# Respacing the filter units of an FFT filter that runs between the matmuls of a GELU MLP

## The chip, the cores and the metric

The kernel runs on one core of a Trainium2 chip. The metric is the time of one execution on the device in microseconds (us), as the median of several runs. A profile is one execution, recorded by the hardware profiler.

## The reference

Eight sequences of 3008 rows and 256 columns are filtered along the rows with a real FFT, a product with a complex filter and the inverse FFT. Each filtered row then goes through an MLP with exact GELU.

```python
X = np.fft.rfft(x, axis=1)                    # x: (8, 3008, 256)
F = (filt_r + 1j * filt_i)[None, :, :]        # (1505, 256)
y = np.fft.irfft(X * F, n=3008, axis=1)
h = y.reshape(24064, 256) @ w_in              # w_in: (256, 2048)
g = 0.5 * h * (1.0 + erf(h / sqrt(2)))
out = g @ w_out                               # w_out: (2048, 256)
```

## The kernel before

**The MLP** is cut into 47 tiles of 512 rows. For each of the 16 blocks of the hidden width, `mm1` (L637) makes two 512-column matmuls into a PSUM bank "h" (three of them), and ScalarE writes the GELU to `g_sb` (L640). The second matmul of a tile, `mm2_seven`, replaces eight block products by seven with sums of its operands: 7 groups m = 0 to 6 of 16 matmuls each (L709), 112 in all. The sums of `g_sb` are made by VectorE in `sums_1` (L678, four a tile), `sums_2` (L684, two) and `sums_3` (L691, two). The results of L709 go into two PSUM banks "o" that alternate: group 0 into one, groups 1 and 2 into the other, 3 and 4 into the first, 5 and 6 into the other. VectorE empties them: L724 after group 0, L726 and L729 after group 2, L731, L732 and L735 after group 4, L738 (two instructions) after group 6. Group 1 of the next tile needs the bank that L738 empties, group 3 the one of L724, group 5 the one of L729.

**The order is a list of slots written out by hand.** Slot s = 16 t + j. In each slot the program first issues what was put there, then 7 matmuls of `mm2_seven` for tile t - 1, then the two matmuls of `mm1` for block j of tile t. So the place of a slot in its tile, j (called phase here), tells which group of L709 runs: group m starts in slot 16 m / 7. Every engine runs its own instructions in this order of issue. Slots 16 to 31 hold a first, plain form of the second matmul (L650, emptied by L654).

**The filter** of batch 0 runs ahead of the slots. Batches 1 to 7 are filtered inside them, each in time for its rows, in steps:

- `fold` (L107, L108): VectorE sums and differences of the loaded rows; four a batch.
- `s1` (L430): 8 matmuls, four a batch; the result goes through `a_sb` to DRAM (`R1`, L439). `r1` (L445) loads it back as `b_sb`, in three loads of 512 KB on the DMA queue of SP.
- `s2` (L457): 32 small matmuls into one bank "h" and three banks "f", for each of three units u. Then `s2_out` (L468), four times a unit: VectorE multiplies a bank with the filter, 128 x 1024 elements, into a tile p. The products are called P1 to P4 here. After P2 and after P4, the same function makes the complex sum of its tile: a subtraction (L471) and an addition (L472).
- `s3` (L485): 24 matmuls of the unit's two tiles p, the first step of the inverse ("inverse burst"), into one bank "h" and the three banks "f". ScalarE empties them (`s3_out`, L326) and SP writes them to DRAM (`R2`, L495). `r2` (L503) loads the result as `d_sb`, four pieces a batch.
- `s4` (L512): 4 matmuls, 16 times a batch, into a bank "f"; ScalarE or VectorE (L326 or L330) writes them to `ring`, where `mm1` reads its rows.
- `load_next`: eight times a batch, the loads of the next batch's rows on the DMA queue of POOL, behind a small copy (`gate`, L146) that waits for one product.

Finished rows leave by `put_rows` (L756) on POOL's queue; of tile 1 three of four pieces go by SP's queue.

**The planner** (the loops over `b` in the kernel's main function) sets the slot of each step from `hi`, the first slot of the first tile that holds rows of batch b: 176, 272, 368, 464, 560 and 656 for b = 2 to 7. In it, `s2` is the triple of slots of the three units, and `s3 = s2[u] + 10` (9 for two units of batch 1). The products stand in slots s2, s2 + 2, s2 + 4 and s2 + 6 (s2, + 2, + 5, + 6 in the second unit of batch 1, one slot later in the first unit of batch 2). `s4` is placed backwards from its due time into slots that are not marked busy, so it moves when `s2` and `s3` move. After the last `s3` of batch b, `after[b]` is the first slot for loads `r2`.

Of the kernel before, what the change touches and what calls it, by code (L numbers as in the profile page):

```python
# [10 lines left out]
ALU = mybir.AluOpType  # L11
# [20 lines left out]
class _Mix:  # L32
# [428 lines left out]
    def s2_out(self, b, u, m, d):  # L461

        if d == 0:
            self.st[b, "p", 2 * u + m] = self.pp.tile([128, 2, 2, 2, 256], BF16, tag="p12", name="p12")
        w, a, v = self.st[b, "p", 2 * u + m], m ^ d, self.nc.vector.tensor_tensor
        ps = self.st[b, "ps2"][m][d].rearrange("p (r c) -> p r c", r=2)
        f = self.Fu[:, :, a, 2 * u + m, :]
        v(out=w[:, a], in0=ps.unsqueeze(2).to_broadcast([128, 2, 2, 256]),  # L468
          in1=f.unsqueeze(1).to_broadcast([128, 2, 2, 256]), op=ALU.mult)
        if d:  # L470
            v(out=w[:, :, 0, 0], in0=w[:, :, 0, 0], in1=w[:, :, 1, 1], op=ALU.subtract)  # L471
            v(out=w[:, :, 0, 1], in0=w[:, :, 0, 1], in1=w[:, :, 1, 0], op=ALU.add)  # L472

    def s3(self, b, u):

# [217 lines left out]
    def mm2_seven(self, t, lo, hi):  # L693

        nc, v = self.nc, self.nc.vector.tensor_tensor
        a11, a12, s2, a22 = self.quarters(t)
        w = self.w_out_sb.rearrange("p (i k) (n o) -> p k n i o", k=2, n=2)
        q = self.w_sums
        s31, s4 = self.st["s", t], self.st.get(("s4", t))
        ops = ((a11, w[:, 0, 0]), (a12, w[:, 1, 0]), (s2, q[:, 1]), (s31[:, :, 0], q[:, 2]),  # L700
               (s31[:, :, 1], q[:, 0]), (a22, q[:, 3]), (s4, w[:, 1, 1]))
        last = t == self.B * self.S // TCH - 1
        for n in range(lo, hi):
            m, sub, i = n // 16, n // 8 % 2, n % 8
            if n % 16 == 0 and (m == 0 or m % 2 == 1) or last and m > 4 and i == 0:
                self.st["o"] = self.bank("ps_o", "h" if n > 80 else "o").rearrange("p (m s o) -> p m s o", m=2, s=2)
            ps = self.st["o"]
            a, b = ops[m]
            nc.tensor.matmul(ps[:, (m + 1) % 2, sub, :], lhsT=a[:, i, 128 * sub:128 * sub + 128], rhs=b[:, i],  # L709
                             start=i == 0, stop=i == 7)  # L710
            if last and m > 4 and i == 7:
                self.finish(t, m, sub, ps)
            if n % 16 != 15 or m % 2 or last and m > 4:
                continue
            p0, p1 = ps[:, 0], ps[:, 1]
            if m == 0:
                self.st["t"] = self.po.tile([128, 2, 2, 128], FP32, tag="ost", name="t_sb")
                self.st["c"] = [None, None]
            if m in (2, 4):
                self.st["c"][m // 4] = self.po.tile([128, 2, 256], FP32, tag="ost", name="ost")  # L720
            t1, t3 = self.st["t"][:, 0], self.st["t"][:, 1]
            c = lambda h, k: self.st["c"][h][:, :, 128 * k:128 * k + 128]
            if m == 0:
                nc.vector.tensor_copy(out=t1, in_=p1)  # L724
            elif m == 2:
                v(out=c(0, 0), in0=t1, in1=p0, op=ALU.add)  # L726
                if last:
                    self.store(t, 0, 0, nc.sync)
                v(out=t1, in0=t1, in1=p1, op=ALU.add)  # L729
            elif m == 4:  # L730
                v(out=t3, in0=t1, in1=p0, op=ALU.subtract)  # L731
                v(out=c(1, 1), in0=t3, in1=p1, op=ALU.add)  # L732
                if last:
                    self.store(t, 1, 1, nc.scalar)
                v(out=t1, in0=t1, in1=p1, op=ALU.add)  # L735
            else:
                for h, tt, p in ((1, t3, p0), (0, t1, p1)):
                    v(out=c(h, 1 - h), in0=tt, in1=p, op=ALU.add)  # L738
                    for sub in range(2):
                        self.put_rows(t * TCH + 256 * h + 128 * sub, self.st["c"][h][:, sub],  # L740
                                      nc.gpsimd if t > 1 or h > sub else nc.sync)

    def put_rows(self, r0, tile_, eng):

# [33 lines left out]
def kernel(  # L778
# [9 lines left out]
    m = _Mix(ctx, tc, x, filt_r, filt_i, moe_w_in, moe_w_out, out)  # L788
    nc, B, S = tc.nc, m.B, m.S
# [116 lines left out]
    def put(slot, f, *a):  # L906
        at.setdefault(slot, []).append((f, a))

    def first(b):
        return (b * S // TCH) * 16  # L910

    busy, crowd, after = set(), set(), {}
    for b in range(1, B):
        hi = first(b)
        e = 4 * (b == B - 1)
        s1, n1, r1 = (4, 2.75, 16) if b == 1 else (hi - 87, 3.7, hi - 73) if b == 2 else (hi - 94 - e, 3.7, hi - 80 - e)
        s2 = (33, 45, 57) if b == 1 else (hi - 64 - 2 * e + (b == 2), hi - 48 - 3 * e + e // 4, hi - 32 - 3 * e)
        busy.update(range(s1 - 1, s1 + int(3 * n1) + 2))
        for c in range(4):
            slot = s1 + int(c * n1 + (b == 1 and c in (1, 2)))  # L920
            put((0, 1, 5, 8)[c] if b == 1 else (67, 69, 86, 94)[c] if b == 2 else s1 - 28 + e + 6 * c, m.fold, b, c)
            put(slot, m.s1, b, c)
        for u in range(3):
            put(r1 if u < 2 else s2[0] + 1, m.r1, b, u)
            put(s2[u], m.s2, b, u)
            for i in range(4):
                put(s2[u] + ((0, 2, 5, 6)[i] if b == u == 1 else 2 * i + (b == 2 and u == 0)), m.s2_out, b, u, i // 2, i % 2)
            s3 = s2[u] + (9 if b == 1 and u != 1 else 10)
            put(s3, m.s3, b, u)
            put(s3 + 1, m.s3_out, b, u, 1)  # L930
            busy.update(range(s2[u] - 1, s2[u] + 5), range(s3 - 1, s3 + 2))
        after[b] = s3 + (5 if b > 1 else 4)
        crowd.update(range(s2[0], after[b]), range(s1 + 66, s1 + 94))
        if b + 1 < B:
            for i, (u, o, p) in enumerate(((0, 5, 1), (0, 7, 1), (1, 1, 2), (1, 5, 3), (1, 7, 3), (2, 1, 4), (2, 5, 5), (2, 7, 5))):
                put(s2[u] + o, m.load_next, b, p, i // 2, i % 2)
# [46 lines left out]
    for s in range((NT + 1) * 16):  # L983
        t, jc = s // 16, s % 16
# [42 lines left out]
```

## Time and profile before

| | us |
|---|---|
| median of 3 runs (750.72 to 751.89) | 751.08 |
| the profiled execution | 750.39 |
| its span, first to last instruction | 748.6 |
| PE busy | 730.8 (98%) |
| DVE (VectorE) busy | 616.9 (82%) |
| ACT (ScalarE) busy | 575.1 (77%) |
| POOL busy | 288.2 (39%) |

In the profile PE is TensorE, PEld its weight loads. A line of the timeline gives start, duration, engine, line of the kernel, operation and operands of an instruction or of equal ones in a row. Instructions of one engine overlap by a little, so a queue without gaps is read by the distance from start to start.

### The profile page before, as it was taken

The page shows a single profiled execution, that of the slowest core. Times are in us where ns is not written, and L with a number is a line of the kernel's source. Part 1 is how long each engine was busy: PE and PEld are TensorE (multiplying, and loading weights), DVE is VectorE, ACT ScalarE, POOL GpSimd, SP SyncE. Part 2 cuts the span into 40 slices and gives each one's busy share as a digit, 9 for nine tenths or more (in the row PEclk, how much of TensorE's full clock was granted, in tenths as well). Part 3 has the DMA queues.
Part 4 walks back from the last instruction along what each step waited for, and adds up shares of the span by engine and source line. Part 5 has one row for each costly group of instructions (what it writes and reads, how often), then busy time and mean ns, then how long its engine had stood idle before and what let it go on. Part 6 is the DMA issues. An engine that isn't in the chain of part 4 may idle for free.

```text
span 748.6 us, 22400 instructions
## 1 busy us (share of the span) xinstructions
PE 730.8 (98%) x9261; PEld 508.9 (68%) x9261; DVE 616.9 (82%) x1120; ACT 575.1 (77%) x1048; POOL 288.2 (39%) x544
## 2 busy tenths in 40 slices
PE   8999999999999999999999999999999999999997
PEld 4856666666777667666677666666767766777776
DVE  8977998899887998789977989769997898676566
ACT  6987777677887788878887777877878787777773
POOL 7893446666122552234431355114631122112121
PEclk9999999999999999999999999999999999999999
DMA  9996542745345552546535455355444433301011
GB/s 154 213 193 185 125 109 86 212 90 123 86 121 177 117 119 82 142 148 134 112 103 162 111 126 131 90 158 129 117 108 118 153 91 99 117 31 58 29 57 58
DMA packets 81353, 89.31 MB, mean 119 GB/s; under 512 B 13171, under 2 KB 60659, under 8 KB 81251
## 3 DMA queue, kind: packets, MB, share of 16 engines
q0 software_dynamic: 22352, 39.76, 23.1%
q1 hardware_dynamic: 58483, 47.93, 22.8%
q8 instruction: 72, 1.18, 0.7%
q14 instruction: 30, 0.25, 0.1%
q10 hardware_dynamic: 416, 0.20, 0.1%
HBM read 55.57 MB, written 48.23 MB: 139 GB/s over the span
## 4 chain that ended last, share of the span: by engine, by line
PE 77%; DVE 15%; DMA 3%; POOL 2%; issue 2%; ACT 0%; DVEq 0%; POOLq 0%; SPq 0%
PE ps_h L637 35%; PE ps_o L709 33%; DVE p L468 5%; DMA x_sb<-in_x_dram 3%; PE ps_s L512 2%; PE ps_s L430 2%; DVE s_sb L678 2%; POOL out_dram L756 1%; PE ps_s L485 1%; DVE p L472 1%; PE ps_s L457 1%; DVE g_sb L684 1%; PE ps_o L650 1%; DVE s_sb L691 1%; DVE x_sb L108 1%
## 5 line engine op out<-in xcount | busy, mean ns | idle before, releaser
L640 ACT ACTIVATE g_sb<-ps_h 128x512 f16<-128x512 f32 x752 | 447.9, 603 | 146.1 <-PE ps_h L637 142.5
L637 PE MATMUL ps_h<-y_sb,w_in_sb 128*128 128x512 bf16 (+3 forms) x1600 | 445.3, 366 | 0.2 <-DVE a_sb L328 0.2
L756 POOL DMA_DIRECT2D out_dram<-ost x228 | 129.4, 574 | 389.3 <-DVE ost L738 359.4
L709 PEld LDWEIGHTS <-g_sb 128*128 128x128 f16 x2944 | 193.9, 98 | 90.1 <-issue 13.5
L709 PEld LDWEIGHTS <-s_sb 128*128 128x128 f16 x2208 | 147.8, 98 | 56.7 <-issue 3.7
L709 PE MATMUL ps_o<-w_sums,g_sb 128*128 128x128 f16 x1472 | 127.5, 219 | 4.7 <-DVE t_sb L729 3.5
L637 PEld LDWEIGHTS <-w_in_sb 128*128 128x128 bf16 x1600 | 125.0, 98 | 8.5 <-issue 1.1
L709 PE MATMUL ps_o<-w_sums,s_sb 128*128 128x128 f16 x1472 | 126.2, 219 | 0.1
L709 PE MATMUL ps_o<-w_out_sb,g_sb 128*128 128x128 f16 x1472 | 119.4, 219 | 2.1 <-DVE ost L738 2.1
L678 DVE TENSOR_TENSOR s_sb<-g_sb 128x1024 f16<-128x1024 f16 x184 | 120.3, 687 | 0.8 <-ACT g_sb L640 0.8
L468 DVE TENSOR_TENSOR p<-ps_s,F 128x1024 bf16<-128x1024 f32 x84 | 102.1, 1217 | 3.5 <-PE ps_s L457 1.8
L99 POOL DMA_DIRECT2D x_sb<-in_x_dram x156 | 79.0, 513 | 2.4 <-DMA x_sb<-in_x_dram 0.8
L684 DVE TENSOR_TENSOR g_sb<-s_sb,g_sb 128x1024 f16<-128x1024 f16 x92 | 65.0, 707 | 1.6
L709 PE MATMUL ps_o<-w_out_sb,s_sb 128*128 128x128 f16 x736 | 63.9, 219 | 0.0
L691 DVE TENSOR_TENSOR s_sb<-g_sb 128x1024 f16<-128x1024 f16 x92 | 63.8, 693 | 0.0
L731 DVE TENSOR_TENSOR t_sb<-t_sb,ps_o 128x256 f32<-128x256 f32 x46 | 19.3, 419 | 40.9 <-PE ps_o L709 39.7
L326 ACT ACTIVATE v_sb<-ps_s 128x512 bf16<-128x512 f32 x83 | 45.5, 608 | 6.3 <-PE ps_s L485 5.7
L326 ACT ACTIVATE y_sb<-ps_s 128x376 bf16<-128x376 f32 x94 | 46.6, 496 | 4.6 <-PE ps_s L512 4.6
L512 PEld LDWEIGHTS <-d_sb 96*128 96x128 bf16 x448 | 31.2, 97 | 27.2 <-issue 2.2
L738 DVE TENSOR_TENSOR ost<-t_sb,ps_o 128x256 f32<-128x256 f32 x90 | 33.7, 415 | 18.1 <-PE ps_o L709 18.1
L328 DVE CAST a_sb<-ps_s 128x512 bf16<-128x512 f32 x54 | 34.7, 684 | 12.7 <-PE ps_s L430 12.4
L726 DVE TENSOR_TENSOR ost<-t_sb,ps_o 128x256 f32<-128x256 f32 x46 | 19.1, 416 | 24.7 <-PE ps_o L709 24.1
(156 smaller groups left out, 556.7 us busy)
## 6 DMA issues: line engine op xcount, KB each, us to landing
out_dram<-ost POOLq DMA_DIRECT2D x126, 128.0 KB, 2.7
b_sb<-R SPq DMA_DIRECT2D x21, 512.0 KB, 5.2
R<-v_sb SPq DMA_DIRECT2D x84, 128.0 KB, 2.6
d_sb<-R SPq DMA_DIRECT2D x56, 192.0 KB, 3.3
R<-a_sb SPq DMA_DIRECT2D x108, 96.0 KB, 2.2
x_sb<-in_x_dram POOLq DMA_DIRECT2D x48, 94.0 KB, 2.7
x_sb<-in_x_dram POOLq DMA_DIRECT2D x48, 48.0 KB, 2.7
x_sb<-in_x_dram POOLq DMA_DIRECT2D x12, 188.0 KB, 5.1
```

The source lines that it names most:

```text
L99: self.nc.gpsimd.dma_start(out=xt[64 * v + to:64 * v + to + m, h, 4 * c:4 * c + 4 * n, :], in_=xv[h][at:at + m, w:w + 4 * n, :])
L326: self.nc.scalar.activation(out=out, in_=in_, func=AF.Copy, scale=1.0 if scale is None else scale)
L328: self.nc.vector.tensor_copy(out=out, in_=in_)
L468: v(out=w[:, a], in0=ps.unsqueeze(2).to_broadcast([128, 2, 2, 256]), in1=f.unsqueeze(1).to_broadcast([128, 2, 2, 256]), op=ALU.mult)
L512: nc.tensor.matmul(ps[:, 94 * i:94 * i + 94], lhsT=d[:, (grp % 2) * 4 + i, 128 * half:128 * half + 128], rhs=self.T4a[:, 4 * grp + i, 0:2 ...
L637: nc.tensor.matmul(ps[:, o:o + n], lhsT=w[:, dc], rhs=self.ring[:, dc, off:off + n], start=(dc == 0), stop=(dc == 1))
L640: nc.scalar.activation(out=self.st["g", t][:, jc, :], in_=ps, func=AF.Gelu)
L678: self.nc.vector.tensor_tensor(out=self.st["s", t][:, i:i + 2], in0=a, in1=b, op=ALU.subtract)
L684: self.nc.vector.tensor_tensor(out=a21[:, k], in0=self.st["s", t][:, k, 0], in1=a22[:, k], op=ALU.add)
L691: self.nc.vector.tensor_tensor(out=self.st["s4", t][:, k], in0=a12[:, k], in1=s2[:, k], op=ALU.subtract)
L709: nc.tensor.matmul(ps[:, (m + 1) % 2, sub, :], lhsT=a[:, i, 128 * sub:128 * sub + 128], rhs=b[:, i], start=i == 0, stop=i == 7)
L756: eng.dma_start(out=out, in_=tile_[lo - r0:lo - r0 + n])
```

## The change

The complex sums leave `s2_out` and become a step of their own, `s2_sum`, one slot behind P2 and one behind P4. The inverse burst stands 13 slots behind its unit (12 in batch 1). The units stand further apart:

| batch | units before | units after | bursts before | bursts after |
|---|---|---|---|---|
| 1 | 33, 45, 57 | 28, 43, 58 | 42, 55, 66 | 40, 55, 70 |
| 2 | 113, 128, 144 | 113, 129, 145 | 123, 138, 154 | 126, 142, 158 |
| 3 to 6 | hi - 64, - 48, - 32 | hi - 72, - 53, - 34 | hi - 54, - 38, - 22 | hi - 59, - 40, - 21 |
| 7 | 584, 597, 612 | 580, 596, 612 | 594, 607, 622 | 593, 609, 625 |

For batches 3 to 6 the phases of the units were 0, 0 and 0; they become 8, 11 and 14. Of batch 1 they were 1, 13 and 9; they become 12, 11 and 10. `r1(b, 2)`, `load_next`, `s4` and `r2` move along, and of the four pieces of tile 1's output one goes by SP's queue instead of three.

```diff
         v(out=w[:, a], in0=ps.unsqueeze(2).to_broadcast([128, 2, 2, 256]),
           in1=f.unsqueeze(1).to_broadcast([128, 2, 2, 256]), op=ALU.mult)
-        if d:
-            v(out=w[:, :, 0, 0], in0=w[:, :, 0, 0], in1=w[:, :, 1, 1], op=ALU.subtract)
-            v(out=w[:, :, 0, 1], in0=w[:, :, 0, 1], in1=w[:, :, 1, 0], op=ALU.add)
+
+    def s2_sum(self, b, p):
+
+        w, v = self.st[b, "p", p], self.nc.vector.tensor_tensor
+        v(out=w[:, :, 0, 0], in0=w[:, :, 0, 0], in1=w[:, :, 1, 1], op=ALU.subtract)
+        v(out=w[:, :, 0, 1], in0=w[:, :, 0, 1], in1=w[:, :, 1, 0], op=ALU.add)
...
-                                      nc.gpsimd if t > 1 or h > sub else nc.sync)
+                                      nc.gpsimd if t > 1 or h * sub == 0 else nc.sync)
...
-        s2 = (33, 45, 57) if b == 1 else (hi - 64 - 2 * e + (b == 2), hi - 48 - 3 * e + e // 4, hi - 32 - 3 * e)
+        s2 = (28, 43, 58) if b == 1 else (hi - 63, hi - 47, hi - 31) if b == 2 else (hi - 72 - e, hi - 53 - 7 * e // 4, hi - 34 - 5 * e // 2)
...
             for i in range(4):
-                put(s2[u] + ((0, 2, 5, 6)[i] if b == u == 1 else 2 * i + (b == 2 and u == 0)), m.s2_out, b, u, i // 2, i % 2)
-            s3 = s2[u] + (9 if b == 1 and u != 1 else 10)
+                put(s2[u] + 2 * i + (b == 2 and u == 0), m.s2_out, b, u, i // 2, i % 2)
+            for i in range(2):
+                put(s2[u] + 3 + 4 * i + (b == 2 and u == 0), m.s2_sum, b, 2 * u + i)
+            s3 = s2[u] + (12 if b == 1 else 13)
...
-        after[b] = s3 + (5 if b > 1 else 4)
+        after[b] = s3 + (5 if 1 < b < B - 1 else 4)
```

Here `e` is 4 for batch 7 and 0 otherwise.

## The prediction

> **What bounds the kernel now.** I read the page's busy times first, then the chain that ended last, then the waits of PE, then the timeline of single units.
>
> ```profile
> PE 730.8 (98%) x9261; PEld 508.9 (68%) x9261; DVE 616.9 (82%) x1120; ACT 575.1 (77%) x1048; POOL 288.2 (39%) x544
> ...
> PE 77%; DVE 15%; DMA 3%; POOL 2%; issue 2%; ACT 0%; DVEq 0%; POOLq 0%; SPq 0%
> ```
>
> PE is the bound, but 15% of the chain is VectorE: in places PE waits for it. How much is read from the slots. Where there is no filter work (660 to 740 us) the `mm1` pairs of neighbouring slots start 0.82 us apart (660.42, 661.24, 662.07), 0.8225 us on average. In the timeline a slot with `s4` is longer by 0.17 us, with `s1` by 0.66, with `s2` by 0.67, with an undisturbed `s3` by 0.68. What a slot takes beyond that is PE's wait. Added up over slots 32 to 640, outside `s1` and tile 5's own slots, the waits are:
>
> | batch | 1 | 2 | 3 | 4 | 5 | 6 | 7 | sum |
> |---|---|---|---|---|---|---|---|---|
> | us | 4.68 | 4.03 | 1.89 | 1.89 | 1.91 | 1.90 | 1.06 | 17.36 |
>
> So 17.4 us is the most that better spacing can bring. In batch 4 the first unit shows where its part comes from. VectorE:
>
> ```profile
> 326.19 0.75 DVE L738 TENSOR_TENSOR ost<-t_sb,ps_o 128x256 f32<-128x256 f32 x2 [0.39 <-PE ps_o L709]
> 327.06 1.22 DVE L468 TENSOR_TENSOR p<-ps_s,F 128x1024 bf16<-128x1024 f32 x1
> 328.20 0.68 DVE L684 TENSOR_TENSOR g_sb<-s_sb,g_sb 128x1024 f16<-128x1024 f16 x1
> ...
> 332.06 0.42 DVE L724 COPY t_sb<-ps_o 128x256 f32<-128x256 f32 x1
> ...
> 335.72 0.42 DVE L472 TENSOR_TENSOR p<-p 128x512 bf16<-128x512 bf16 x1
> 336.05 0.41 DVE L726 TENSOR_TENSOR ost<-t_sb,ps_o 128x256 f32<-128x256 f32 x1
> ```
>
> From 327.06 VectorE has no gap for 9 us. L724 ends at 332.48 and PE's group 3 starts at 332.53, 0.17 us late; the last sum (L472) ends at 336.14 and the burst pays 0.29. But L738 stands **ahead** of the first product, and is in time. That is what phase 0 gives. A unit at phase 8 is in the trace too, the first of batch 7:
>
> ```profile
> 591.44 1.22 DVE L468 TENSOR_TENSOR p<-ps_s,F 128x1024 bf16<-128x1024 f32 x1 [0.87 <-PE ps_s L457]
> ...
> 593.18 1.22 DVE L468 TENSOR_TENSOR p<-ps_s,F 128x1024 bf16<-128x1024 f32 x1
> 594.43 0.42 DVE L471 TENSOR_TENSOR p<-p 128x512 bf16<-128x512 bf16 x1
> ...
> 600.48 0.69 DVE L678 TENSOR_TENSOR s_sb<-g_sb 128x1024 f16<-128x1024 f16 x1
> 601.09 0.74 DVE L738 TENSOR_TENSOR ost<-t_sb,ps_o 128x256 f32<-128x256 f32 x2
> ```
>
> ```profile
> 600.87 0.28 PE L709 MATMUL ps_o<-w_out_sb,g_sb 128*128 128x128 f16 x2
> 601.88 0.44 PE L709 MATMUL ps_o<-w_out_sb,g_sb 128*128 128x128 f16 x5 [0.73 <-DVE ost L738]
> ```
>
> Here L738 stands **behind** the whole unit. PE, two matmuls into the slot, has to wait for its bank: 0.89 us. Of all empties L738 has the least time: its data is ready at the end of a tile and group 1 wants the bank 2.3 slots (1.9 us) later. The others have 4.6 slots.
>
> **The change part by part.** It adds and removes no arithmetic, no matmul and no byte. The sums run one slot later in the list, but where VectorE has a queue, place in the list is only order. So each unit is a sum of VectorE's queue against PE's time. Steps in a full queue, start to start: product 1.14 us, complex sum 0.68 (0.11 more directly behind its product), L678, L684 and L691 0.60 (0.72 for an L684 that needs the one before), L731 to L735 1.11, L724 0.33, L738 0.66, from L738's last start group to PE's restart 0.79 in all (601.09 to 601.88).
>
> *Phase 8, first units of batches 3 to 6.* Between P1 and the L738 of their tile the queue is the same as in the unit of batch 7 above: 4 products, 2 sums, one L691, L731 to L735, three L678, then L738: 4.56 + 1.58 + 0.60 + 1.11 + 1.80 + 0.79 = 10.44 us, which is 591.44 to 601.88. PE gets to group 1 sooner, though: in batch 7 its way held the burst (0.68, and 0.17 of wait) and two `s4`; now the burst is 13 slots off, behind that point, and one `s4` is left. Late by 0.89 + 0.68 + 0.17 + 0.17 = **1.91 us**.
>
> *Phase 11, second units.* P1, L731 to L735, two L678, P2, sum, P3, one L678, L738: 3.42 + 1.11 + 1.80 + 0.68 + 0.79 = 7.80 us. PE needs 7 slots and 0.14: 5.90. Late by 1.90. Then P4 stands ahead of the second L684: L684, P4, L678, L684 end 3.07 us after PE's restart, and group 2's fifth matmul wants them after 2.42: 0.65 more. **2.55 us**.
>
> *Phase 14, third units.* L738 comes second and is in time. The second L684 ends 6.28 us after P1's start, PE wants it at 6.02 (0.17 sooner in batches 5 and 6, which have no `s4` there); L724 behind P3 ends at 7.76, wanted at 7.37 counting that wait. **0.65 us**, 0.82 in batches 5 and 6. Against 0.98 to 1.34 now: a gain.
>
> So batches 3 to 6 wait 5.11, 5.11, 5.28, 5.28: 20.8 us in place of 7.6. The bursts themselves, 2.7 us of wait in these batches, wait for nothing any more.
>
> *Batch 1* (phases 12, 11, 10). The first unit starts P1 at 61.40 (slot 28 starts at 60.76, and its `b_sb` landed at 59.62). The first L684 then ends at 68.64, wanted at 67.54: 1.10; the second 0.66; L724 0.38. The second unit: 2.55 as above. The third: L738 1.06, L684 1.43. Sum 7.2; the burst four slots later moves `d_sb` towards the first `s4` in slot 82 (landed 11.9 us after the burst's matmuls; 10.5 now left, but ScalarE will not be held up): 0.3, bounds 0 and 2. **7.5 in place of 4.68**.
>
> *Batch 2* (phases 1). The unit moves a slot off L738 and the burst three: second and third units wait 0 to 0.1, against 0.45 and 1.34. In the first unit `s4` waits for P3's and P4's banks, 2.1 us as now. **2.15 in place of 4.03**. *Batch 7* (phases 4): the pattern of its present second and third units, with no waits: **0 in place of 1.06**.
>
> *What the earlier units ask of the DMA.* `b_sb` must be there 8 slots sooner (4 in batch 7). `r1` cannot be issued sooner: it waits for the writes of `s1`. The page:
>
> ```profile
> b_sb<-R SPq DMA_DIRECT2D x21, 512.0 KB, 5.2
> ```
>
> The first loads landed at 232.29, 321.31, 410.40, 501.07 and 587.95 in batches 3 to 7; the new slots start at 229.4, 319.7, 410.0, 500.3 and 587.2 on the same clock. Late by 2.9, 1.6, 0.4, 0.8, 0.8. In batches 3 and 4 two `d_sb` loads ran beside them that now go before (`r2` moves from slot 189 to 183, 285 to 279), and the undisturbed loads took 3.8 us: nothing, then. I take **2.4 us**; bounds 0 and 6.5. `r1(b, 2)` now stands ahead of the next `r2` in SP's queue and holds it until `s2` has freed a buffer; that `d_sb` is wanted 13 slots later. On POOL the copies (`gate`) wait for P1 or P3, which are queued already; out rows behind them have 11 slots. Tile 1's two pieces move to POOL, idle there. Nothing for these, cover lost at worst 1 us. The last loads of batch 7 have 4.9 us of slack and lose 2.5.
>
> Sum: 7.5 + 2.15 + 20.8 + 0 + 2.4 = 32.85 of waits in place of 17.36: **+15.5 us**. On the profiled execution, 750.39 (span 748.6 and 1.8 around it), that is 765.9; the median of runs is 0.69 above that execution: 766.6.
>
> The longest wait so far, 1.85 us before 153.63, left the granted clock at 1.00 (150 to 156 us). [...]
>
> **Rivals.** (1) *Waits only change places*, 753 to 759: a unit's excess of VectorE work over PE's time is paid once, at the burst or at L738, so the new ones replace the old. For it: total work is equal. Against it: the excess at phase 0 lands on L724, with 4.6 slots of slack, and the burst. Price: loads 2.4, and of the other 13.1 us half at most. (2) *Faster*, 738: VectorE empties L738 in time and bursts and groups wait no more. It decides at 8.5 us of queue between P1 and L738 in the first unit, against my 10.4; then only batch 1's last, batch 2's and the loads stay, 5 us for 17.4. For it: three more slots are 2.5 us, more than any burst waits. Against: 591.44 to 601.88 is measured, and the order of the changed program puts L738 behind P4 and P3. (3) *No change within 0.2%*: the gains of batches 2, 7 and the bursts offset L738. (4) *Slower still*, 773 or more: loads at 6.5, and each long wait delays the next.
>
> **How the numbers follow.** My sum 0.70 (761 to 772); rival 1 0.10; rival 2 0.06; rival 3 0.03; rival 4 0.11. The range 757 to 773 leaves out the last of the slow and the fast; its low end is no wait for loads (-2.4) and eight waits smaller by 0.9, its high end all loads late. Faster by over 0.2%, about what a measurement can tell from no change, 0.06; within it 0.04; slower 0.90.
>
> **What would show it.** In the new profile PE waits for the two empties that are L738 here in slots 210, 226, 306, 322 and so on, some 1.9 us each, eight times in batches 3 to 6; bursts of 0.68 us; none of these in batch 7. P1 of first units in batches 5 to 7 begins late by `b_sb`. I am wrong if those empties end before group 1's slot, or if the waits are under 1 us.

## The result, and the profile after

The changed kernel takes 768.26 us (median of 4 runs, 766.33 to 768.87); before, next to it on the same chip, takes 750.92 (4 runs). The ratio is 1.0224, with an interval of 1.0202 to 1.0245: **17.3 us slower**. The profiled execution is 768.87 with a span of 767.1, 18.5 more than that of before.

In the changed kernel and in the kernels derived from it, lines after 470 are three higher: L709 is L712, L724 is L727, L729 is L732, L738 is L741, L684 is L687, the burst is L488, the sums are L474 and L475. On the page, the busy times and the chain:

```profile
PE 726.7 (95%) x9261; PEld 506.2 (66%) x9261; DVE 611.6 (80%) x1118; ACT 574.2 (75%) x1050; POOL 289.9 (38%) x547
...
PE 61%; DVE 23%; DMA 8%; ACT 3%; issue 3%; SPq 1%; POOL 1%; DVEq 0%; POOLq 0%; ACTq 0%
```

PE, VectorE and ScalarE are busy for a little less time than before, POOL, with two more of tile 1's pieces, for 1.7 us more. The chain lost 16 points of PE to VectorE (+8), DMA (+5) and ScalarE (+3): PE waits more often. For what, the waits of PE tell (bank, then releaser; total us, times, longest):

```profile
PE ps_o L712 <- DVE ost L741: 17.4, 11, 1.8
PE ps_o L712 <- DVE g_sb L687: 6.2, 12, 1.1
PE ps_s L457 <- DMA b_sb<-R: 4.0, 4, 1.8
```

Nothing here is a burst. Eleven times group 1 waits for L741, 1.6 us on average. One of them is the first unit of batch 4, VectorE first:

```profile
333.27 1.28 DVE L681 TENSOR_TENSOR s_sb<-g_sb 128x1024 f16<-128x1024 f16 x2
334.47 1.22 DVE L468 TENSOR_TENSOR p<-ps_s,F 128x1024 bf16<-128x1024 f32 x1
335.73 0.43 DVE L474 TENSOR_TENSOR p<-p 128x512 bf16<-128x512 bf16 x1
336.07 0.42 DVE L475 TENSOR_TENSOR p<-p 128x512 bf16<-128x512 bf16 x1
336.40 0.69 DVE L681 TENSOR_TENSOR s_sb<-g_sb 128x1024 f16<-128x1024 f16 x1
337.00 0.75 DVE L741 TENSOR_TENSOR ost<-t_sb,ps_o 128x256 f32<-128x256 f32 x2
```

then PE in the same stretch:

```profile
335.34 0.59 PE L640 MATMUL ps_h<-y_sb,w_in_sb 128*128 128x512 bf16 x2
335.78 0.28 PE L712 MATMUL ps_o<-w_out_sb,g_sb 128*128 128x128 f16 x2
337.81 0.45 PE L712 MATMUL ps_o<-w_out_sb,g_sb 128*128 128x128 f16 x5 [1.76 <-DVE ost L741]
```

P4 (334.47) and its sum stand ahead of L741 in a queue without a gap; PE has done its two matmuls of group 0 at 336.06 and goes on at 337.81. Read from the slots as the prediction does, this wait is 1.93 us. All waits, by batch, before and after:

| batch | 1 | 2 | 3 | 4 | 5 | 6 | 7 | sum |
|---|---|---|---|---|---|---|---|---|
| before | 4.68 | 4.03 | 1.89 | 1.89 | 1.91 | 1.90 | 1.06 | 17.36 |
| predicted, without loads | 7.5 | 2.15 | 5.11 | 5.11 | 5.28 | 5.28 | 0 | 30.4 |
| after, without loads | 7.05 | 3.01 | 5.12 | 5.12 | 5.12 | 5.12 | 0 | 30.5 |
| after, for `b_sb` | 0 | 0 | 0.78 | 0.48 | 0.14 | 1.88 | 1.18 | 4.46 |

Together 35.0 in place of 17.4, +17.6. Tile 5 has 0.18 more, the start up to slot 27 took 0.98 longer in this execution, the end after the last slot 0.37 less; that leaves 0.1 of the 18.5 open.

### The profile page after: what moved, and what is told of

It is laid out like the page before. It is cut to its first block, busy times and chain, and to the rows that moved or that the text cites. A ratio compares the mean times of both kernels' runs of the same rounds, so it can differ in the third digit from the quotient of the medians.

```text
span 767.1 us, 22403 instructions
## 1 busy us (share of the span) xinstructions
PE 726.7 (95%) x9261; PEld 506.2 (66%) x9261; DVE 611.6 (80%) x1118; ACT 574.2 (75%) x1050; POOL 289.9 (38%) x547
## 3 DMA queue, kind: packets, MB, share of 16 engines
q8 instruction: 72, 1.18, 0.7%
## 4 chain that ended last, share of the span: by engine, by line
PE 61%; DVE 23%; DMA 8%; ACT 3%; issue 3%; SPq 1%; POOL 1%; DVEq 0%; POOLq 0%; ACTq 0%
PE ps_h L640 27%; PE ps_o L712 25%; DVE p L468 9%; DVE s_sb L681 5%; DMA b_sb<-R 3%; DMA R<-a_sb 3%; DVE g_sb L687 2%; PE ps_s L515 2%; PE ps_s L488 1%; DVE ost L741 1%; PE ps_s L430 1%; PE ps_s L457 1%; DVE p L475 1%; ACT a_sb L326 1%; ACT g_sb L643 1%
## 5 line engine op out<-in xcount | busy, mean ns | idle before, releaser
L712 PEld LDWEIGHTS <-g_sb 128*128 128x128 f16 x2944 | 194.2, 98 | 111.5 <-DVE ost L741 19.3
L759 POOL DMA_DIRECT2D out_dram<-ost x231 | 131.4, 575 | 333.6 <-DVE ost L741 325.0
L712 PEld LDWEIGHTS <-s_sb 128*128 128x128 f16 x2208 | 147.2, 98 | 57.2 <-issue 8.4
L712 PE MATMUL ps_o<-w_out_sb,g_sb 128*128 128x128 f16 x1472 | 120.7, 219 | 17.4 <-DVE ost L741 17.4
L712 PE MATMUL ps_o<-w_sums,g_sb 128*128 128x128 f16 x1472 | 129.4, 219 | 6.6 <-DVE g_sb L687 6.2
L712 PE MATMUL ps_o<-w_sums,s_sb 128*128 128x128 f16 x1472 | 126.2, 219 | 0.9 <-DVE t_sb L727 0.9
L687 DVE TENSOR_TENSOR g_sb<-s_sb,g_sb 128x1024 f16<-128x1024 f16 x92 | 65.4, 712 | 1.5
L712 PE MATMUL ps_o<-w_out_sb,s_sb 128*128 128x128 f16 x736 | 63.9, 219 | 0.0
L146 POOL COPY gate<-p 1x1 bf16<-1x1 bf16 x48 | 15.7, 327 | 124.0 <-DVE p L468 123.9
L326 ACT ACTIVATE y_sb<-ps_s 128x376 bf16<-128x376 f32 x96 | 47.5, 495 | 4.5 <-PE ps_s L515 4.5
L326 ACT ACTIVATE v_sb<-ps_s 128x512 bf16<-128x512 f32 x83 | 45.5, 608 | 0.4 <-PE ps_o L712 0.3
L741 DVE TENSOR_TENSOR ost<-t_sb,ps_o 128x256 f32<-128x256 f32 x90 | 33.7, 417 | 10.3 <-PE ps_o L712 10.3
```

What stands on the lines that cost most here:

```text
L326: self.nc.scalar.activation(out=out, in_=in_, func=AF.Copy, scale=1.0 if scale is None else scale)
L687: self.nc.vector.tensor_tensor(out=a21[:, k], in0=self.st["s", t][:, k, 0], in1=a22[:, k], op=ALU.add)
L759: eng.dma_start(out=out, in_=tile_[lo - r0:lo - r0 + n])
```

## The experiments

The kernels are numbered in the order of the runs. Kernel 5 has the lines of before, 4, 6 and 11 one more than after, 8, 9 and 12 two more; outside the lines shown, the text uses the line numbers of after for them. `...` marks lines left out. Each kernel ran next to before on one chip; before had a median between 750.75 and 750.90 in all of them (7 or 8 runs each).

**1. Units of batches 3 to 6 back at phase 0.**

```diff
-        s2 = (28, 43, 58) if b == 1 else (hi - 63, hi - 47, hi - 31) if b == 2 else (hi - 72 - e, hi - 53 - 7 * e // 4, hi - 34 - 5 * e // 2)
+        s2 = (28, 43, 58) if b == 1 else (hi - 63, hi - 47, hi - 31) if b == 2 else (hi - 72 - e, hi - 53 - 7 * e // 4, hi - 34 - 5 * e // 2) if b == B - 1 else (hi - 64, hi - 48, hi - 32)
...
-            s3 = s2[u] + (12 if b == 1 else 13)
+            s3 = s2[u] + (12 if b == 1 or 2 < b < B - 1 else 13)
```

> After, with the units of batches 3 to 6 back at phase 0 (hi - 64, - 48, - 32) and their bursts 12 slots behind them; batches 1, 2 and 7 and the split sums stay as after. My theory (the phase of a unit in its tile decides): the waits at L741 and L687 and the late b_sb of batches 3 to 6 go, 23.8 us in all; what stays of them is the wait at the third unit's L729/L732 and L727, about 0.8 to 1.2 a batch. So 768.3 - 19 to 20.5, 748 to 749.5 us. Rival 1 (waits only change places; the spacing did not cost it, but the split sums or the later bursts): 760 or more.

747.05 us, 0.9947 (0.9932 to 0.9962) of before. The spacing of these twelve units is worth 21.2 us, more than the whole loss; what is left of the change is a small gain. The waits of batches 3 to 6 are 0.58, 0.58, 0.92 and 0.92, all at the third unit's empties after group 2:

```profile
PE ps_o L712 <- DVE t_sb L732: 2.3, 4, 0.7
```

None is for L741 or for `b_sb` in these batches, nor for `b_sb` in batch 7.

**2. P4 behind L741.** First units of batches 3 to 6, P4 at s2 + 8, its sum at s2 + 9.

```diff
-                put(s2[u] + 2 * i + (b == 2 and u == 0), m.s2_out, b, u, i // 2, i % 2)
+                put(s2[u] + 2 * i + (b == 2 and u == 0) + 2 * (2 < b < B - 1 and u == 0 and i == 3), m.s2_out, b, u, i // 2, i % 2)
...
-                put(s2[u] + 3 + 4 * i + (b == 2 and u == 0), m.s2_sum, b, 2 * u + i)
+                put(s2[u] + 3 + 4 * i + (b == 2 and u == 0) + 2 * (2 < b < B - 1 and u == 0 and i == 1), m.s2_sum, b, 2 * u + i)
```

> After, with P4 and its sum of the first unit of batches 3 to 6 two slots later, so that they stand behind both L741 of their tile in VectorE's queue. My theory: one product and one sum less ahead of L741, 1.14 + 0.68 = 1.82 us less of a wait of 1.93: four waits shrink to about 0.1, 7.3 us less, 761 us. Rival (waits only change places): P4 then delays another empty or the burst by as much, 766 to 768.

762.58 us (1.0157, 1.014 to 1.0174), 5.7 less than after, between the two. PE's waits:

```profile
PE ps_o L712 <- DVE ost L741: 10.4, 7, 1.7
PE ps_o L712 <- DVE g_sb L687: 8.1, 16, 1.2
```

Four of the eleven waits for L741 are gone, whole, which is what my theory says. Four others have come: 0.645 us each in slots 213, 309, 405 and 501, for the second L687 (16 times in place of 12). P4 has left the queue ahead of L741 and stands ahead of L687 now, which PE, no longer held up, wants at once. PE in slots 212 and 213:

```profile
243.96 0.33 PE L712 MATMUL ps_o<-w_sums,g_sb 128*128 128x128 f16 x3
244.13 0.38 PE L640 MATMUL ps_h<-y_sb,w_in_sb 128*128 128x512 bf16 x1
244.66 0.64 PE L488 MATMUL ps_s<-p,U 32*64 32x256 bf16 x32
245.23 0.23 PE L712 MATMUL ps_o<-w_sums,g_sb 128*128 128x128 f16 x1
245.93 0.51 PE L712 MATMUL ps_o<-w_sums,g_sb 128*128 128x128 f16 x6 [0.47 <-DVE g_sb L687]
```

So 7.7 us went and 2.6 came back: a third of what was pushed back moved to the next taker. The waits for `b_sb` were 2.4 us in this execution, without an edit to them.

**3. Loads of batches 4 to 6 sooner.**

```diff
-        s1, n1, r1 = (4, 2.75, 16) if b == 1 else (hi - 87, 3.7, hi - 73) if b == 2 else (hi - 94 - e, 3.7, hi - 80 - e)
+        s1, n1, r1 = (4, 2.75, 16) if b == 1 else (hi - 87, 3.7, hi - 73) if b == 2 else (hi - 98, 3.7, hi - 84) if 3 < b < B - 1 else (hi - 94 - e, 3.7, hi - 80 - e)
...
```

The second edit, left out here, keeps the folds in their slots.

> After, with s1 and r1 of batches 4 to 6 four slots (3.3 us) sooner and the folds where they were. My theory: the waits of s2 for b_sb in batches 4, 5 and 6 (0.48, 0.14 and 1.88 us) go and nothing takes their place: 2.5 us less, 765.8. Rival (the start of the unit is not what is late; the unit's queue then ends as late as before): 768.

766.08 us, 2.2 less than after, whose own four runs spread over 2.5 us, so the traces carry this reading and not the medians. The waits for `b_sb` in batches 4 to 6 are zero and nothing else changed there: 5.12 in each. Batches 3 and 7, not touched, have 0.62 and 0.79.

**4. The sums alone a slot later**, in the kernel before.

```diff
-        if d:
-            v(out=w[:, :, 0, 0], in0=w[:, :, 0, 0], in1=w[:, :, 1, 1], op=ALU.subtract)
-            v(out=w[:, :, 0, 1], in0=w[:, :, 0, 1], in1=w[:, :, 1, 0], op=ALU.add)
...
+    def s2_sum(self, b, p):
...
+            for i in (1, 3):
+                put(s2[u] + 1 + ((0, 2, 5, 6)[i] if b == u == 1 else 2 * i + (b == 2 and u == 0)), m.s2_sum, b, 2 * u + i // 2)
```

> Before, with the complex sums alone a slot behind P2 and P4; units, bursts and loads as before. My theory (in a full queue a place in the list is only order): within 1.5 us of before, 749.5 to 752; the 0.11 us of a sum directly behind its product is saved 42 times off the path, and the last sum, one slot later, may hold the burst by up to 0.5 us where something is queued between. Rival (the split sums carry part of the loss): 754 or more.

762.28 us (1.0155, 1.0133 to 1.0177): **11.5 us slower, where I expected nothing.**

```profile
PE ps_s L489 <- DVE p L475: 14.6, 16, 1.9
```

It is the bursts that wait, for the last sum. (A burst has 32 matmuls in the traces, where the description of the kernel before says 24.) The third unit of batch 5 shows why, VectorE:

```profile
464.34 1.22 DVE L468 TENSOR_TENSOR p<-ps_s,F 128x1024 bf16<-128x1024 f32 x1
465.47 0.68 DVE L107 TENSOR_TENSOR xs<-x_sb 111x1024 bf16<-111x1024 bf16 x1
...
466.80 0.41 DVE L730 TENSOR_TENSOR ost<-t_sb,ps_o 128x256 f32<-128x256 f32 x1
467.24 0.42 DVE L733 TENSOR_TENSOR t_sb<-t_sb,ps_o 128x256 f32<-128x256 f32 x1
467.58 0.42 DVE L475 TENSOR_TENSOR p<-p 128x512 bf16<-128x512 bf16 x1
467.92 0.42 DVE L476 TENSOR_TENSOR p<-p 128x512 bf16<-128x512 bf16 x1
```

and PE:

```profile
465.75 0.42 PE L489 MATMUL ps_s<-p,U 32*64 32x256 bf16 x16
468.05 0.65 PE L489 MATMUL ps_s<-p,U 32*64 32x256 bf16 x16 [1.88 <-DVE p L475]
```

One slot is one place in the list, but what stood in that place, a fold and the two empties after group 2, is 2.1 us of VectorE. In units without a fold it is 0.78, and most of their bursts wait 0.99 us in place of 0.29.

**5. The bursts alone two slots later**, in the kernel before.

```diff
-            s3 = s2[u] + (9 if b == 1 and u != 1 else 10)
+            s3 = s2[u] + (12 if b > 1 else 9 if u != 1 else 10)
```

> Before, with the bursts of batches 2 to 7 alone moved, from 10 to 12 slots behind their units; units, joined sums and batch 1 as before. My theory: each burst of before that waited (2.76 us in batches 3 to 6, 0.96 in batch 2, 1.06 in batch 7) waits no more, since VectorE's queue is through with the unit by then; the wait at the third unit's L729, which PE now reaches up to 0.3 us sooner, grows by 0.3 in five batches at most. 4.8 us less, 1.5 at most back: 746 to 747.5. Rival (the same excess is paid at the next empty): 750 to 751.

755.95 us (1.0069, 1.0052 to 1.0085): slower too, by 5.2. No burst of batches 2 to 6 waits, as expected, but:

```profile
PE ps_o L709 <- DVE t_sb L729: 8.4, 12, 1.5
```

In before this bank was waited for 0.87 us in the third unit, and not at all in the others; now 1.5 to 1.7 there and 0.18 to 0.35 in the others. A burst that stands ahead of group 5 is 0.68 us of PE's own work and, where it waits, more: time in which VectorE gets to L729. With the burst behind it, group 5 asks sooner by all that. I had counted only the 0.3 us of wait, not the burst itself, although the prediction makes this very step for L738 (where PE's way lost 0.68 of burst). Batch 7 has the same: L738 is 1.76 us late in slot 594 now that the burst there is gone, and 1.54 are new in slot 597, where `s2` waits until ScalarE (L326) has emptied the banks of the burst one slot before.

**6. Batch 1 alone as after.** The kernel before, and for b = 1 also the split sums.

```diff
-        s2 = (33, 45, 57) if b == 1 else (hi - 64 - 2 * e + (b == 2), hi - 48 - 3 * e + e // 4, hi - 32 - 3 * e)
+        s2 = (28, 43, 58) if b == 1 else (hi - 64 - 2 * e + (b == 2), hi - 48 - 3 * e + e // 4, hi - 32 - 3 * e)
...
-            s3 = s2[u] + (9 if b == 1 and u != 1 else 10)
+            s3 = s2[u] + (12 if b == 1 else 10)
```

> Before, with batch 1 alone as in after (units at 28, 43, 58, its sums a slot behind, its bursts 12 slots behind). My theory: the waits of batch 1 are 7.05 us in the trace of after and 4.68 in that of before: 2.4 us more, 753.2. If the start before slot 28, 1.0 us longer in after's profile, belongs to this change too: 754.1. Rival (the longer way of batch 1 is made up before tile 5): 751.

753.12 us (1.0032, 1.0019 to 1.0045), 2.37 over before; the traces give 7.05 - 4.68 = 2.37. A longer start is not needed for that, but the interval, 1.4 to 3.4 us, does not exclude one. With the same steps ahead of it in all kernels, `mm1` of slot 27 began between 60.3 and 61.3 us (mean 60.6) in the profiled executions of the seven kernels that have batch 1 as before, and between 61.0 and 61.8 (mean 61.5) in the seven that have it as after. So after's 0.98 us are in part spread; whether the change lengthens the start as well stays open.

**7. P4 behind L741 and the first bursts later still**, s2 + 15. The two edits of kernel 2, and:

```diff
-            s3 = s2[u] + (12 if b == 1 else 13)
+            s3 = s2[u] + (12 if b == 1 else 13) + 2 * (2 < b < B - 1 and u == 0)
```

> Like the kernel with P4 of the first unit two slots later, and the first units' bursts of batches 3 to 6 another two slots later as well (15 behind the unit). My theory: the 0.64 us that these four bursts waited for the later sum go, and nothing else changes: 2.6 us less than that kernel's 762.6, 760.0. Rival (the excess of a unit must be paid somewhere): the next empty takes it, 762 to 763.

765.75 us (1.019, 1.0169 to 1.0212), 3.2 more than kernel 2. The expectation rested on a misreading: I had taken the 0.645 us of slot 213 for the burst's, since the slot holds it. It was L687's, behind the burst:

```profile
243.12 0.33 PE L515 MATMUL ps_s<-T4a,d_sb 96*128 96x94 bf16 x4
243.29 0.22 PE L712 MATMUL ps_o<-w_sums,g_sb 128*128 128x128 f16 x1
244.49 0.51 PE L712 MATMUL ps_o<-w_sums,g_sb 128*128 128x128 f16 x6 [0.98 <-DVE g_sb L687]
```

With the burst gone from that slot (0.68) and an `s4` in its place (0.17), PE asks for L687 0.51 us sooner: 0.645 + 0.51 = 1.15, and 1.15 it is in all four batches. That is 2.0 us, as in kernel 5 not a price of VectorE's but of PE's own work that went behind the wait. The other 1.2 are not explained; the profiled execution (762.89) was the fastest of the four.

**10. P3 behind L741 in the second units.** P3 at s2 + 5, P4 at s2 + 7, P4's sum at s2 + 8, batches 3 to 6.

```diff
-                put(s2[u] + 2 * i + (b == 2 and u == 0), m.s2_out, b, u, i // 2, i % 2)
+                put(s2[u] + 2 * i + (b == 2 and u == 0) + (2 < b < B - 1 and u == 1 and i > 1), m.s2_out, b, u, i // 2, i % 2)
...
-                put(s2[u] + 3 + 4 * i + (b == 2 and u == 0), m.s2_sum, b, 2 * u + i)
+                put(s2[u] + 3 + 4 * i + (b == 2 and u == 0) + (2 < b < B - 1 and u == 1 and i > 0), m.s2_sum, b, 2 * u + i)
```

> After, with P3 and P4 of the second unit of batches 3 to 6 and P4's sum one slot later. P3 then stands behind both L741 of its tile, P4 behind both L687. My theory (what stands ahead of an empty in VectorE's queue sets the wait): the four waits of 1.91 us before group 1 shrink by a product, 1.14 us each, and the wait for the second L687 stays at 0.5 to 0.65, since P3 has taken P4's place ahead of it: 4.6 us less, 763.7. Rival (what a unit has too much is paid somewhere): the bursts or later empties take it, 766 to 768.

763.78 us (1.0174, 1.0149 to 1.0198), 4.5 less than after.

```profile
PE ps_o L712 <- DVE ost L741: 12.8, 11, 1.8
...
PE ps_o L712 <- DVE t_sb L727: 1.3, 7, 0.2
```

The four waits of the second units fell from 1.91 to 0.78, by 1.13 us, one product; the wait for L687 stayed at 0.65 and 0.48. But L727, which now stands behind P4, is 0.35 and 0.18 late, 1.06 in all, so a quarter came back, and 0.7 of the saving by the traces was `b_sb`, not this edit. The sum came out nearer than its parts.

**11. Sums and bursts together**, kernels 4 and 5 in one.

> Before with both of the parts that were tried alone: all sums a slot behind, and the bursts of batches 2 to 7 12 slots behind their units; units, folds and loads as before. Alone the sums cost 11.5 us and the bursts 5.2. My theory (the sum that goes behind the empties after group 2 frees these, if the burst does not ask for it at once): each cures the other's wait. Batches 3 to 6 wait 3.0 us as with the units put back, not 7.6; batch 2 about 2.5, not 4.0; batch 7 keeps the 3.3 us that the later bursts gave it, not 1.06. 747 us. Rival (the two costs add): 767.

746.92 us (0.9952, 0.9935 to 0.9969). Alone they cost 11.5 and 5.2, together they gain 4.0. VectorE in the third unit of batch 4 of kernel 5, where the sum (L471, L472) is ahead:

```profile
365.78 1.22 DVE L468 TENSOR_TENSOR p<-ps_s,F 128x1024 bf16<-128x1024 f32 x1
367.03 0.42 DVE L471 TENSOR_TENSOR p<-p 128x512 bf16<-128x512 bf16 x1
...
367.71 0.68 DVE L107 TENSOR_TENSOR xs<-x_sb 111x1024 bf16<-111x1024 bf16 x1
...
369.49 0.42 DVE L729 TENSOR_TENSOR t_sb<-t_sb,ps_o 128x256 f32<-128x256 f32 x1
```

and of kernel 11:

```profile
361.23 1.22 DVE L468 TENSOR_TENSOR p<-ps_s,F 128x1024 bf16<-128x1024 f32 x1
362.37 0.68 DVE L107 TENSOR_TENSOR xs<-x_sb 111x1024 bf16<-111x1024 bf16 x1
...
364.14 0.42 DVE L733 TENSOR_TENSOR t_sb<-t_sb,ps_o 128x256 f32<-128x256 f32 x1
364.48 0.42 DVE L475 TENSOR_TENSOR p<-p 128x512 bf16<-128x512 bf16 x1
```

From P4's start to the empty L729 (L733) it is 3.71 us in the one and 2.91 in the other: the empties that PE wants next go first, the sum that nobody wants before the burst goes behind. That works only if the burst can wait. Waits per batch in batches 3 to 6: before 1.89 to 1.91; sums alone 3.96 (5.60 in batch 5); bursts alone 2.53 to 2.63; both 0.58 to 0.92.

**8, 9, 12. What the runs recommend, gathered.** Against before, kernel 12 has: the split sums in batches 2 to 7, bursts at + 12 (+ 13 in batch 2's first unit), from after the queues of tile 1's output and `after[b]`, and

```diff
-        s2 = (33, 45, 57) if b == 1 else (hi - 64 - 2 * e + (b == 2), hi - 48 - 3 * e + e // 4, hi - 32 - 3 * e)
+        s2 = (33, 45, 57) if b == 1 else (hi - 75, hi - 59, hi - 44) if b == B - 1 else (hi - 64 + (b == 2), hi - 48 + (b == 2), hi - 32)
...
-            put((0, 1, 5, 8)[c] if b == 1 else (67, 69, 86, 94)[c] if b == 2 else s1 - 28 + e + 6 * c, m.fold, b, c)
+            put((0, 1, 5, 8)[c] if b == 1 else (67, 69, 86, 94)[c] if b == 2 else s1 + e + (-25, -16, -11, -7)[c], m.fold, b, c)
...
-            busy.update(range(s2[u] - 1, s2[u] + 5), range(s3 - 1, s3 + 2))
+            busy.update(range(s2[u] - 1, s2[u] + 5 + 4 * (b == 2 and u == 0)), range(s3 - 1, s3 + 2))
```

Kernel 8 was the first form (units of batch 7 at 580, 596 and 612 with bursts at + 13, second unit of batch 2 at 128, and only the first fold moved), kernel 9 the second (581, 596, 612; 129; folds as above). From 8 to 9:

```diff
-        s2 = (33, 45, 57) if b == 1 else (hi - 76, hi - 60, hi - 44) if b == B - 1 else (hi - 64 + (b == 2), hi - 48, hi - 32)
+        s2 = (33, 45, 57) if b == 1 else (hi - 75, hi - 60, hi - 44) if b == B - 1 else (hi - 64 + (b == 2), hi - 48 + (b == 2), hi - 32)
...
-            put((0, 1, 5, 8)[c] if b == 1 else (67, 69, 86, 94)[c] if b == 2 else s1 - 28 + e + 6 * c + 3 * (c == 0), m.fold, b, c)
+            put((0, 1, 5, 8)[c] if b == 1 else (67, 69, 86, 94)[c] if b == 2 else s1 + e + (-25, -16, -11, -7)[c], m.fold, b, c)
```

> All that the runs so far recommend: batch 1 as before; batches 2 to 6 in before's phases (0 or 1), with the split sums and bursts 12 slots behind (13 in the first unit of batch 2); batch 7 as after; no s4 in the four slots in which the first unit of batch 2 holds its banks; and the first fold of each batch from the third on three slots later, behind the empties after group 2 of the third unit. My theory: the waits left are batch 1's 4.7 us and tile 5's 1.9, about 0.5 elsewhere, 7 in place of 19: 739 us. Rival (the folds and s4 that move cost their time at another empty): 744 to 747.

742.22 us (0.9885, 0.987 to 0.99). 3 us short of the forecast: L741 (L743 in this kernel) behind a fold in slots 162, 258 and their like (0.21 to 0.55), banks in slot 128 (0.72), `b_sb` of batch 7 (1.12).

> The gathered version with three waits taken up that its trace still shows: the second to fourth fold of each batch from the third on go 2 to 6 slots later, so that none stands ahead of L741 in slots 162, 258, 354 and so on (0.21 to 0.55 us each); the second unit of batch 2 goes one slot later (its s2 waited 0.72 us for the banks of the burst before it); the first unit of batch 7 goes one slot later (its b_sb came 1.12 us late). My theory: about 0.6 + 1.5 + 0.7 + 0.8 = 3.6 us less than 742.2, 738.6. Rival (the folds push another empty or s1 back by as much): 741 to 743.

739.46 us (0.9854, 0.9839 to 0.9869). Those waits are gone; one of 0.72 is new, in slot 596, where `s2` follows a burst after two slots.

> The last gathered version with the second unit of batch 7 one slot later and its bursts 12 slots behind instead of 13. The 0.72 us that s2 waited in slot 596, two slots behind a burst whose banks it needs, go; nothing else changes: 738.7. Rival (the earlier bursts wait for their sums): 739.5 to 741.

**738.67 us** (738.60 to 738.87), 0.9837 (0.9822 to 0.9851) of before: 12.2 us faster than before, 29.6 below after's median. On its page:

```profile
PE 724.2 (98%) x9261; PEld 506.9 (69%) x9261; DVE 612.3 (83%) x1119; ACT 574.2 (78%) x1049; POOL 292.4 (40%) x547
...
PE 86%; DVE 6%; DMA 3%; POOL 2%; issue 1%; ACT 0%; DVEq 0%; POOLq 0%
```

VectorE's share of the chain fell from 15% to 6%. Batches 3 to 7 have no wait left; batch 1 has its 4.7 and tile 5 its 1.9.

## Why the prediction was right, and where it was not

It forecast 766.6; the median is 768.26. Step by step:

- **First units (phase 8), 1.91 us each: right.** 1.93 in slots 210, 306, 402 and 498. Kernel 1 removes it by the phase, kernel 2 by taking P4 out of the queue ahead of L741.
- **Second units (phase 11), 1.90 + 0.65: right** in batches 3 and 4 (1.91 + 0.65), 0.16 too much in batches 5 and 6 (0.48 at L687). Kernel 10 moved the first part by one product, as its working says.
- **Third units (phase 14), 0.65 and 0.82: right** (0.63 and 0.80).
- **Bursts and batch 7's units wait for nothing: right**; the slots of all bursts have no excess.
- **Batch 1, 7.5: 7.05.** By unit 2.04, 2.51 and 2.50 against 2.14, 2.55 and 2.5; the 0.3 us for `d_sb` did not come.
- **Batch 2, 2.15: 3.01.** The step that failed is "second and third units wait 0 to 0.1". I followed VectorE's queue to the end of the unit and not to the next L741. Batch 3's folds stand there, one ahead of P4 (186.78) and one between its sum and L741 (192.54), and L741 was 0.90 us late in slot 162.
- **Loads, 2.4: 4.46, within the bounds of 0 to 6.5.** The step that failed is "the undisturbed loads took 3.8 us: nothing, then" for batches 3 and 4: with the `d_sb` loads out of their way the first loads still took 5.4 us (227.35 to 232.80) and 5.1; what slowed them stays open. In batch 6 three of the last four writes of `s1` took 3.9 to 4.3 us, where those of batch 4 took 1.9 to 2.3, and the fourth was issued 2.5 us behind the third, at 509.31, so that the load was issued only at 512.11. Also, the term's own parts (0, 0, 0.4, 0.8, 0.8) add up to 2.0 and not to 2.4. In kernels 2, 7 and 10, which have the same loads, these waits were 2.4, 2.0 and 3.8: the term is a spread, not a number.
- **The sum of the other waits, 30.4 against 30.5, is nearer than its parts**, by luck: batch 2 is 0.86 over the forecast, batch 1 0.45 under it, batches 5 and 6 together 0.32 under it.
- **"Where VectorE has a queue, place in the list is only order"**: true, and I drew no price from it. The split of the sums, taken alone, costs 11.5 us; I did not see it, and expected nothing of kernel 4. The forecast was not hurt, because with the bursts 12 or 13 slots behind their units the sums were never the last. Two of the edits help each other and gain 4.0 us; it is the spacing of batches 3 to 6 that loses 21.2.
- **No term for the granted clock in the sum: right.** It is at 1.00 in every window of 10 us of after from 60 to 760 us. Kernel 4 shows that this was not safe: there, in batches 2 and 5, a wait of 1.88 us was followed by 3.4 us at 0.50; see the last section.

The rivals: that waits only change places (1) fails for the whole, 17.3 us against 2 to 8, but the runs show it in parts: a third of what was pushed back came back in kernel 2, a quarter in kernel 10. Rivals 2 and 3 fell with the 1.93 us for L738, rival 4 with the loads, which were late by 4.5 and not 6.5. Not settled are 1.2 us of kernel 7, and why the start up to slot 27 varies by 1.5 us between executions.

## What to carry to other kernels

A stage has a due time for each of its results, and where the queue is worked off in the order of issue, as VectorE's is in every stretch shown here, moving a unit means changing which due times it stands ahead of (in the first units, P4 and its sum ahead of L741 go with 1.76 us of wait in after, behind it with none in kernel 2): look for the result with the least slack (here L738, 1.9 us where the others have 3.8) and keep long instructions behind it. Price each edit alone before pricing the sum: two that lose 11.5 and 5.2 us alone gained 4.0 together, since each took away the other's wait. And when a block of the bounding engine's own work is moved behind a wait, look for that block in the wait: in kernel 7 the wait grew from 0.645 to 1.15 us, by the 0.68 of the burst less the 0.17 of the `s4` in its place.

## What the runs showed of the hardware

Kernel 4's wait of 1.88 us in the third unit cost more in batch 5 than in batch 6. The granted clock is why; in windows of 2 us around the burst shown above (its length, PE's busy time with its instructions, then the clock, DMA share and GB/s):

```profile
466.00:468.00 2.00, 0.17 (x16) 1.00 0.82 121
468.00:470.00 2.00, 1.88 (x30) 0.89 0.33 56
470.00:472.00 2.00, 2.00 (x17) 0.50 0.51 113
472.00:474.00 2.00, 2.00 (x20) 0.76 0.17 42
```

In windows of 0.2 us the clock is 0.86 in the one from 469.40, then 0.50, 0.61 in the one from 472.80, then 1.00: it falls to 0.50 at 469.54, 1.5 us after PE's restart at 468.05, and is back at 1.00 at 472.96, after 3.42 us at half speed. The three slots from 469.04 to 473.32 took 4.28 us, where two plain ones and one with `s4` take 2.64 by the slot lengths of before (0.8225 us, and 0.17 for `s4`). Waits and slowed slots of batch 5 add to 5.60 us, those of batch 6, with the same pause, to 3.96. The same happened in batch 2, from 189.65 to 193.06, after a pause of the same 1.88 us. This execution was the slowest of the kernel's four, 764.72 us at a mean granted clock of 0.996; in the others the mean was 0.998 to 0.999, so not each of them had both stretches (3.41 and 3.42 us at 0.50 take 0.0045 off the mean of a span of 762.9). In batch 6 the clock stayed at 1.00, as it did after the pauses of 1.54 us in batches 3 and 4 and after's eight of 1.74 to 1.76 for L741. One thing that differs between after's pauses and kernel 4's is what stands around them: in kernel 4 the pause lies inside a burst of 32-row matmuls, 16 ahead of it and 16 behind, so that PE ran no 128-row matmul for 2.9 us (465.75 to 468.63). But that pause is also longer, 1.88 us against 1.76, and no run separates the two. Neither tells batch 6 from batches 2 and 5: there, too, the pause was 1.88 us with 16 matmuls of the burst on either side (559.72 and 562.03). What does is not shown, nor how short a pause can be and still have such a fall behind it.

A second thing is the spread of the DMA: the first `b_sb` loads (512 KB) of batches 3 to 6 landed after 3.7 to 5.4 us in one execution of after, and the same unedited loads made PE wait 2.0 to 4.5 us in all from one kernel to the next. Kernel 12, in whose trace no unit waits for a load, spread over 0.3 us in four runs, after over 2.5. The loads alone do not explain that: in the traces of kernels 1, 9 and 11 no unit waits for a load either, and their runs spread over 1.8, 2.2 and 1.4 us.
